# Low halves of the second weight matrix: one VectorE operation in place of a scaled copy on ScalarE and a subtraction on GpSimd

## The chip, the core and the metric

The kernel runs on one core of a Trainium2 chip. The metric is device time in microseconds (us) of one execution, the median of several runs. The engines are named as in the profile: PE (TensorE, matmuls), PEld (its weight loads), DVE (VectorE), ACT (ScalarE), POOL (GpSimd), SP (SyncE, which issues all DMAs here). Each engine works through its own queue in order; semaphores make one wait for another.

## The reference

Local and global attention, then a Fourier mixing layer, then a two-layer network with residual:

```python
s_g  = scale * q_g @ k_all^T;  out_g = softmax(s_g) @ v_all          # 32 global rows
s_ll = where(|i-j| <= 32, scale * q_l @ k_l^T, -1e9)                 # 512 local rows, a band
out_l = softmax([scale * q_l @ k_g^T, s_ll]) @ [v_g, v_l]
x  = heads of [out_g, out_l] side by side                             # (8, 544, 512)
u  = x + real(fft(fft(x, axis=1), axis=2))
un = (u - mean(u)) / sqrt(var(u) + 1e-6)
out = u + max(un @ w_ch1, 0) @ w_ch2                                  # 512 -> 2048 -> 512
```

The weights are drawn in double precision (`w_ch1` is 512 x 2048, `w_ch2` 2048 x 512); there are 8 batches, 8 heads and a head width of 64.

## The kernel before, in words

**Number format.** PE multiplies float16. Each float32 operand is carried as two float16 tiles, a high half (the value rounded) and a low half (what the rounding left), and each product is the sum of three: high x high, high x low, low x high. So for most operands there are a scaling, a high half and a low half to make, on ACT, DVE or POOL.

**Stages.** Per pair of heads: load q, k, v, sum their absolute values for a scale (`sums`, `scales`, tile `z`), split them (`prep_mul`, `prep_hi`, `prep_lo`, `v_mul`, `v_hi`, `v_lo`), local scores on PE (`scores`, L398), mask with running minimum on DVE (`masked`, L408), exponential on ACT (`exps`, L417), split of the probabilities (`p_hi` on ACT, `p_lo` on POOL, L425), a transposing DMA (`turn`), values on PE (`values`, L446, L448), normalisation on DVE (`norm`). The global rows go the same way (`g_scores`, `g_max`, `g_exp`, ...). Per batch the Fourier mixing follows: rows are loaded, folded by symmetry (`d_tail`, `d_even` on DVE, `d_odd` on POOL), split (`d_hi`, `d_lo`, the latter L636 on DVE) and multiplied with tables on PE. Then the network runs in 17 blocks of 256 rows: statistics (`l_stats`), normalised rows and their halves (`l_un`, `l_lo`), a transposing DMA, 8 steps of `f_first` (L811), `f_hi` (ACT), `f_lo` (DVE, L820) and `f_second` (L830), and at the end `f_end` (DVE, L835), which adds the residual.

**The weights.** They come as 64-bit numbers, 32 tiles of 128 x 512, and are turned into float32 with bit operations on DVE (`w_abs`, `w_bits`), into tiles `wm`. `w_max`, `w_fold` and `w_scale` find scales, which are powers of two, in tile `wsc`. `w_split` makes the float16 halves of tile `i` of matrix `k` (0 for `w_ch1`, 1 for `w_ch2`, called w2) into `wh`: `w_hi` writes the high half on ACT (L252). For w1 POOL then scales the float32 tile (L259) and subtracts (L262). For w2 ACT scales it in place (L261) and POOL subtracts (L262). w2's tiles are called split 0 to split 15 here. The slots of `wm` and `wh` rotate in one pool of 18: the `wh` of a w2 split takes the place that `wm` had two splits before.

**The order.** Every piece of work has a time in a plan (`Plan.add`, in slots of one quarter of a head pair, with a rank inside a slot), and the whole program is written out in the order of these times; nothing reorders it afterwards. `w_split` of w2 has slot 33 to 48 with rank .75: in a slot it comes after the masks (.67) and the global maximum (.68), and in ACT's queue after nearly all of the slot's other work. From slot 37 on the steps of the network's first block are woven in. `f_second(0, fp)` is the first reader of w2's halves 2fp and 2fp + 1.

Of the kernel before, what the change touches and what calls it, by code (L numbers as in the profile page):

```python
# [13 lines left out]
AF = mybir.ActivationFunctionType  # L14
ALU = mybir.AluOpType
# [75 lines left out]
class Kern:  # L91
# [163 lines left out]
    def w_split(self, k, i):  # L255
        nc = self.nc
        f, s, w = self.w_hi(k, i)
        if k == 0:
            nc.gpsimd.tensor_mul(f, f, s.to_broadcast([P, 512]))  # L259
        else:  # L260
            nc.scalar.activation(f, f, AF.Copy, scale=s)  # L261
        nc.gpsimd.tensor_sub(w[:, 1], f, w[:, 0])  # L262

    def b_load(self, b):
# [774 lines left out]
```

## Time and profile before

| what | us |
|---|---|
| median of 3 runs (lowest, highest) | 1156.88 (1155.44, 1157.02) |
| the profiled execution's own time | 1152.42 |
| its span, first to last instruction | 1150.5 |
| PE busy | 962.0 (84%) |
| DVE busy | 708.7 (62%) |
| ACT busy | 633.6 (55%) |
| POOL busy | 575.1 (50%) |
| mean granted TensorE clock | 0.941 |

The profile is one execution. Its page gives busy time by engine, the span in 40 slices, the chain of work that ended last, and groups of instructions by source line; other views give the busy time in chosen stretches, the waits, and the single instructions in order of time. A row of such a timeline reads: start in us, duration in us, engine, line, operation, output and inputs, and in brackets the idle time of the engine before it with what ended that wait. A duration includes any time for which the instruction was held after its start. The average shares hide that the stages differ: w1's and w2's weights are prepared and the first batches' attention runs in the first 300 us, and the network's matmuls fill the rest.

### The profile page before, as it was taken

How to read it: one execution, taken by the hardware profiler on the slowest of the kernel's cores; microseconds unless marked ns; L12 is line 12 of the kernel's file. 1: busy time of each engine (PE TensorE's matmuls, PEld its weight loads, DVE VectorE, ACT ScalarE, POOL GpSimd, SP SyncE). 2: the span in 40 equal slices, each digit the busy share in tenths (PEclk: the TensorE clock that was granted, in tenths of full speed). 3: DMA queues.
4: the chain of work that ended last, by engine and by line, in shares of the span. 5: the costliest groups of instructions: out<-in, count | busy, mean ns of one | idle time of the engine just before them, and what ended most of it. 6: DMA issues, size and time to landing. Idle time of an engine off the chain costs nothing.

```text
span 1150.5 us, 25346 instructions
## 1 busy us (share of the span) xinstructions
PE 962.0 (84%) x9831; PEld 682.0 (59%) x9831; DVE 708.7 (62%) x1868; ACT 633.6 (55%) x1366; POOL 575.1 (50%) x728
## 2 busy tenths in 40 slices
PE   0244226588799899999999999999999999999996
PEld 0133215465576677676766676767677666666664
DVE  6997798547866865686568656866584444413211
ACT  5768558888676656665666566656564213212210
POOL 3789375778656554665465546654573312201100
PEclk9996557699899999999999999999999999999999
DMA  7578966567387465747465746573646212011100
GB/s 267 151 152 225 276 157 141 112 135 170 75 179 151 108 167 91 141 115 165 93 138 118 170 88 143 112 179 72 135 79 130 60 58 65 24 46 38 19 19 19
DMA packets 249569, 137.63 MB, mean 120 GB/s; under 512 B 200576, under 2 KB 223200, under 8 KB 249448
## 3 DMA queue, kind: packets, MB, share of 16 engines
q1 hardware_dynamic: 249448, 136.01, 51.2%
q8 instruction: 77, 1.26, 0.5%
q14 instruction: 44, 0.36, 0.1%
HBM read 65.10 MB, written 18.35 MB: 73 GB/s over the span
## 4 chain that ended last, share of the span: by engine, by line
PE 55%; DVE 24%; ACT 8%; DMA 6%; POOL 4%; issue 2%; SPq 0%; DVEq 0%; POOLq 0%; ACTq 0%
PE ps L811 22%; PE acc L830 22%; PE S L398 2%; DMA xt<-xs 2%; ACT pe L417 2%; DVE pe L408 2%; DMA qk<-in_qk 2%; PE bk L707 2%; DVE h L820 1%; PE S L468 1%; DVE ps L195 1%; DVE ps L196 1%; DVE z L328 1%; DVE wm L197 1%; DVE ps L194 1%
## 5 line engine op out<-in xcount | busy, mean ns | idle before, releaser
L811 PE MATMUL ps<-uh,wh 128*128 128x256 f16 x3264 | 383.4, 275 | 0.0
L830 PE MATMUL acc<-wh,h 128*128 128x512 f16 x1632 | 377.3, 381 | 4.1 <-DVE u L835 2.9
L811 PEld LDWEIGHTS <-wh 128*128 128x128 f16 x3264 | 319.2, 99 | 59.4 <-issue 0.7
L830 PEld LDWEIGHTS <-h 128*128 128x128 f16 x1632 | 153.5, 99 | 174.1 <-issue 9.2
L820 DVE SCALAR_TENSOR_TENSOR h<-ps,h 128x512 f16<-128x512 f32 x136 | 93.3, 686 | 188.6 <-ACT h L816 188.0
L425 POOL TENSOR_TENSOR ph<-pe,ph 128x448 f16<-128x448 f32 x128 | 137.2, 1072 | 143.0 <-ACT ph L421 88.5
L816 ACT ACTIVATE h<-ps 128x512 f16<-128x512 f32 x136 | 80.2, 589 | 223.4 <-PE ps L811 223.3
L417 ACT ACTIVATE pe<-pe,nm 128x224 f32<-128x224 f32 x256 | 102.0, 469 | 72.1 <-DVE nm L408 71.8
L408 DVE CUSTOM_DVE_ANT_0 pe<-S,msk,z 128x224 f32<-128x224 f32 x256 | 99.6, 445 | 7.5 <-PE S L398 3.6
L446 PE MATMUL bk<-vN,pl 128*128 128x65 f16 x768 | 72.9, 203 | 31.9 <-DMA pl<-ph 10.0
L398 PE MATMUL S<-kT,qT 64*128 64x192 f16 x768 | 55.7, 269 | 44.1 <-ACT pg L482 37.5
L398 PEld LDWEIGHTS <-qT 64*128 64x128 f16 x1536 | 53.7, 101 | 49.7 <-issue 38.9
L446 PEld LDWEIGHTS <-pl 128*128 128x128 f16 x768 | 62.2, 104 | 23.9 <-DMA pl<-ph 18.4
L421 ACT ACTIVATE ph<-pe 128x448 f16<-128x448 f32 x128 | 72.0, 562 | 0.0
L448 PEld LDWEIGHTS <-pl 96*128 96x128 f16 x768 | 60.1, 104 | 17.3 <-issue 10.5
L764 POOL TENSOR_SCALAR ve<-ve 128x2 f32<-128x2 f32 x17 | 5.8, 339 | 113.3 <-DVE ve L763 113.1
L376 POOL TENSOR_TENSOR kT<-qk,kT 128x512 f16<-128x512 f32 x32 | 40.7, 1272 | 36.4 <-ACT kT L371 33.0
L723 DVE SCALAR_TENSOR_TENSOR asm<-bk,dsc,asm 128x258 f32<-128x258 f32 (+1 forms) x21 | 10.1, 482 | 75.1 <-PE bk L707 60.5
L448 PE MATMUL bk<-vB,pl 96*128 96x65 f16 x576 | 55.2, 204 | 0.0
L774 ACT ACTIVATE un<-u,ve 128x512 f32<-128x512 f32 x34 | 27.6, 811 | 47.7 <-DVE unh L779 37.7
L361 ACT ACTIVATE qk<-qk,z 128x512 f32<-128x512 f32 x64 | 45.2, 708 | 10.7 <-DVE z L326 10.7
L262 POOL TENSOR_TENSOR wh<-wm,wh 128x512 f16<-128x512 f32 x32 | 38.0, 1188 | 19.7 <-ACT wm L261 18.3
(188 smaller groups left out, 1654.8 us busy)
## 6 DMA issues: line engine op xcount, KB each, us to landing
qk<-in_qk SPq DMA_DIRECT2D x32, 512.0 KB
vf<-in_v SPq DMA_DIRECT2D x32, 320.0 KB
raw<-in_moe_w_ch SPq DMA_DIRECT2D x18, 512.0 KB
xs<-x SPq DMA_DIRECT2D x32, 256.0 KB
out<-u SPq DMA_DIRECT2D x16, 512.0 KB
rw<-in_moe_w_ch SPq DMA_DIRECT2D x12, 512.0 KB
x<-xs SPq DMA_DIRECT2D x24, 256.0 KB
u<-xs SPq DMA_DIRECT2D x24, 256.0 KB
```

Of the source, the lines that this page charges most:

```text
L361: self.nc.scalar.activation(s[nm], s[nm], AF.Copy, scale=s["z"][:, 3:4] if nm == "q" else s["z"][:, 4:5])
L398: nc.tensor.matmul(ps, qT[r, a, j], k, start=m == 0, stop=m == 2)
L408: nc.vector.tensor_tensor_reduce(self.per[(4 * p + j) % 4][:, h, 0:224], S[:, h, 224 * n:224 * n + 224], self.msk[:, j], z[:, 8:9], 3e38, ...
L417: nc.scalar.activation(pe[:, h, 0:224], pe[:, h, 0:224], AF.Exp, bias=nm[:, n, h:h + 1], scale=-1.0)
L421: self.nc.scalar.activation(ph[:, 0, :, 0:224], self.per[i % 4][:, :, 0:224], AF.Copy)
L425: self.nc.gpsimd.tensor_sub(ph[:, 1, :, 0:224], self.per[i % 4][:, :, 0:224], ph[:, 0, :, 0:224])
L446: nc.tensor.matmul(pv[:, j % 2, h], pl[:, 4 * a + 2 * h], vN[:, j, c, h, :], start=m == 0, stop=False)
L448: nc.tensor.matmul(pv[:, j % 2, h], pl[0:96, 4 * a + 2 * h + 1], vb, start=False, stop=m == 2)
L811: nc.tensor.matmul(ps[:, q], wt[:, w, c0:c0 + P], uh[:, :, 4 * a + kt, :], start=n == 0, stop=n == 11)
L816: self.nc.scalar.activation(h[:, 0], self.fps, AF.Relu)
L820: self.nc.vector.scalar_tensor_tensor(h[:, 1], self.fps, 0.0, h[:, 0], op0=ALU.max, op1=ALU.subtract)
L830: nc.tensor.matmul(self.acc_f[j], h[:, a, q, j * P:(j + 1) * P], self.w[1, f][:, w, :], start=f == 0 and a == 0 and w == 0, stop=f == 15 a ...
```

## The change

For w2 alone, the low half is made in one operation on DVE, `(f * s) - hi`, from the float32 tile, the scale and the high half. The scaled copy in place on ACT and the subtraction on POOL are no longer made. The high half on ACT and all of w1 stay.

```diff
         if k == 0:
             nc.gpsimd.tensor_mul(f, f, s.to_broadcast([P, 512]))
         else:
-            nc.scalar.activation(f, f, AF.Copy, scale=s)
+            nc.vector.scalar_tensor_tensor(w[:, 1], f, s, w[:, 0], op0=ALU.mult, op1=ALU.subtract)
+            return
         nc.gpsimd.tensor_sub(w[:, 1], f, w[:, 0])
```

In the changed kernel every line after the change has a number higher by one (L262 for w1 is L263 there, L820 is L821).

Three places show what moves. On POOL, the stretch around splits 1 and 2, before the change (kT is the low half of k, vN of v, ph of the probabilities):

```order
L732 TENSOR_TENSOR xm<-xm,asm 15x255
L262 TENSOR_TENSOR wh<-wm,wh 128x512
L425 TENSOR_TENSOR ph<-pe_89,ph 128x2x224
L262 TENSOR_TENSOR wh<-wm,wh 128x512
L376 TENSOR_TENSOR kT_66<-qk,kT_66 128x512
L351 TENSOR_TENSOR vN<-vf_76,vN 128x5x2x64
L425 TENSOR_TENSOR ph<-pe_86,ph 128x2x224
L791 TENSOR_TENSOR ve<-ve 128x2
```

and with it:

```order
L733 TENSOR_TENSOR xm<-xm,asm 15x255
L426 TENSOR_TENSOR ph<-pe_89,ph 128x2x224
L377 TENSOR_TENSOR kT_66<-qk,kT_66 128x512
L352 TENSOR_TENSOR vN<-vf_76,vN 128x5x2x64
L426 TENSOR_TENSOR ph<-pe_86,ph 128x2x224
L792 TENSOR_TENSOR ve<-ve 128x2
```

The two subtractions are gone, and the rest stands as it was. On DVE, splits 3 and 4 with the change (dng and xg are the normalisation of global rows, h the low half of the network's inner layer, dn of local rows):

```order
L261 SCALAR_TENSOR_TENSOR wh<-wm,wsc,wh 128x512
L512 TENSOR_SCALAR dng<-bk_127,z 64x1
L513 RECIPROCAL dng<-dng 64x1
L514 TENSOR_SCALAR xg<-bk_127,dng 64x64
L261 SCALAR_TENSOR_TENSOR wh<-wm,wsc,wh 128x512
L821 SCALAR_TENSOR_TENSOR h<-ps_2449,h 128x512
L458 TENSOR_SCALAR dn<-bk_128,z 128x4
```

Before, the same rows followed each other without the two L261. Last, on DVE at splits 13 and 14, in the folding of the second batch for its Fourier mixing (st, xt, et, x) and the global maximum (ng):

```order
L261 SCALAR_TENSOR_TENSOR wh<-wm,wsc,wh 128x512
L644 TENSOR_TENSOR st<-xt 32x255
L645 TENSOR_TENSOR xt<-xt 32x255
L646 TENSOR_TENSOR et<-xt 32x129
L647 TENSOR_TENSOR et<-xt 32x128
L648 TENSOR_TENSOR et<-st 32x128
L649 TENSOR_TENSOR et<-st 32x128
L598 TENSOR_TENSOR x_3160<-x_3160 128x4x255
L600 TENSOR_TENSOR x_3160<-x_3160 128x2x257
L475 TENSOR_REDUCE ng<-S 64x1
L476 TENSOR_REDUCE ng<-S 64x1
L477 TENSOR_SCALAR ng<-ng,z 64x1
```

Split 13's operation now stands ahead of the folding, and split 14's comes right behind the last of these rows.

## The prediction

> **What bounds the kernel now.** First the table of busy time by stretch (columns: stretch in us, length, busy us and instructions of PE, PEld, DVE, ACT, POOL, then granted clock, DMA share, GB/s), cut where w2's sixteen tiles are split.
>
> ```profile
> 200.00:220.00 20.00, 6.96 (x91) 5.43 (x92) 13.12 (x42) 14.94 (x29) 13.16 (x16) 0.57 0.68 134
> 220.00:240.00 20.00, 17.58 (x229) 13.57 (x224) 7.68 (x30) 19.36 (x42) 16.90 (x26) 0.92 0.62 143
> 240.00:260.00 20.00, 16.89 (x176) 11.66 (x175) 12.19 (x37) 16.15 (x37) 13.77 (x14) 0.91 0.49 106
> 260.00:280.00 20.00, 19.64 (x237) 14.36 (x235) 13.88 (x45) 18.47 (x39) 16.51 (x25) 1.00 0.67 160
> 280.00:300.00 20.00, 12.67 (x124) 8.14 (x124) 17.46 (x29) 16.38 (x36) 18.52 (x18) 0.83 0.49 93
> 400.00:600.00 200.00, 194.94 (x2103) 138.38 (x2101) 131.12 (x360) 123.58 (x277) 111.22 (x147) 0.99 0.59 127
> ```
>
> From 400 us on PE is busy 97% of the time (194.94 of 200): nothing but PE sets the pace there, and what arrives earlier at that stage ends earlier. From 200 to 300 us it is otherwise. The five rows sum to 73.7 us of PE, 64.3 of DVE, 85.3 of ACT and 78.9 of POOL in 100 us. ACT is the fullest, POOL next, and PE stands idle for 26 us. Next, the two instructions that the change takes away (duration minimum/median/maximum, first and last start).
>
> ```profile
> L261 ACT ACTIVATE wm<-wm,wsc x16: 721/722/724, 207.4 to 295.4; 128x512 f32<-128x512 f32 x16
>   POOL wh L262: 18.3, 9
> L262 POOL TENSOR_TENSOR wh<-wm,wh x32: 1145/1157/2151, 32.0 to 296.2; 128x512 f16<-128x512 f32 x32
> ```
>
> All sixteen L261 lie in that stretch, and in 9 cases POOL's subtraction L262 stood still until its L261 was done, 18.3 us together. So ACT's scaled copy holds up ACT's own queue and POOL's. Last, the chain that ended last, in order of time: two of its stretches.
>
> ```profile
> 217.43 0.72 ACT wm L261
> 218.15 0.67 ACT pg L481
> ...
> 219.13 1.30 PE S L398 x19
> ...
> 230.43 0.72 ACT wm L261
> ```
>
> The copy stands on the path that sets the end, ahead of the scores that PE waits for.
>
> **The change part by part.** It removes 16 L261 on ACT (16 x 0.722 = 11.6 us busy) and 16 L262 on POOL (16 x 1.157 = 18.5 us), and adds 16 operations on DVE, each f*s - hi from two SBUF tiles, 128x512 f32 to f16. That operation with these operands is in the profile: L636, the lower half of the DFT input.
>
> ```profile
> L636 DVE SCALAR_TENSOR_TENSOR eh<-s,dsc,eh x8: 732/744/1525, 173.2 to 957.8; 128x512 f16<-128x512 f32 x8
> 299.37 1.05 DVE L636 SCALAR_TENSOR_TENSOR eh<-x,dsc,eh 128x514 f16<-128x514 f32 x1
> 299.83 1.49 POOL L425 TENSOR_TENSOR ph<-pe,ph 128x448 f16<-128x448 f32 x1
> ```
>
> Alone it takes 0.74 us; its longest took 1.53. The two rows under it show why: DVE's operation overlaps POOL's, both are long. I take 1.0 us as the price of one, between 0.74 and 1.53, nearer the lower since POOL loses a quarter of its work here; 16 us of DVE in all, bounds 11.9 and 24.4. DVE goes from 64 to about 80 us in 100. [...]
>
> What is saved on the path, stretch by stretch. (A) Before 219 us:
>
> ```profile
> 217.43 0.72 ACT L261 ACTIVATE wm<-wm,wsc 128x512 f32<-128x512 f32 x1
> 218.06 0.76 ACT L481 ACTIVATE pg<-S,ng,z 64x512 f32<-64x512 f32 x1
> 218.29 1.15 POOL L262 TENSOR_TENSOR wh<-wm,wh 128x512 f16<-128x512 f32 x1 [2.77 <-ACT wm L261]
> ```
>
> From start to start the copy costs ACT 218.06 - 217.43 = 0.63 us; the exponential behind it releases PE's scores. Gain 0.63. The earlier splits 0 and 1 fall where ACT still waits on DVE, and I count nothing: split 0's new operation stands ahead of the DFT chain on DVE (+0.74), but L734 below is slow, most likely beside POOL's L340 of that time, which moves away when the L262 ahead of it goes.
>
> ```profile
> L733 DVE TENSOR_TENSOR xf<-xf,asm 18x257 f32<-18x257 f32 x8 | 3.7, 463 | 0.0
> 209.69 1.46 DVE L734 TENSOR_TENSOR xf<-xf,asm 18x255 f32<-18x255 f32 x1
> ```
>
> Its sister L733 of two more columns has a mean of 0.46 us (the upper row: busy us, mean ns); so 1.46 - 0.46 = 1.0 can come back there. Bounds -0.3 to +1.0 net.
>
> (B) From 219 to 245 us. POOL is behind, and PE waits for POOL:
>
> ```profile
> 226.12 1.15 POOL L262 TENSOR_TENSOR wh<-wm,wh 128x512 f16<-128x512 f32 x1
> 227.24 1.15 POOL L376 TENSOR_TENSOR qT<-qk,qT 128x512 f16<-128x512 f32 x1
> 228.45 0.26 PE L398 MATMUL S<-kT,qT 64*128 64x192 f16 x2 [2.10 <-POOL qT L376]
> ```
>
> POOL loses two L262 ahead of this qT (at 218.29, with its 2.77 us of waiting, and at 226.12): up to 2.77 + 2 x 1.15 = 5.1 us, of which some is spent on waiting for ACT's ph in between. More than 2.10 stays, and PE's wait goes. PE's gain is at most 0.63 + 2.10 = 2.7 at 229 us. ACT has to follow: three copies in its unbroken row between 224.7 and 239 us, one of them the 230.43 of the chain above, give 3 x 0.63 = 1.9. The smaller holds: B = 1.9. DVE has room: it is busy 7.68 of 20 us there, and splits 3 to 7 stand in its gaps. If ACT did not follow at all (its exponentials wait for DVE's masks), B would be 0; with all of PE's wait it is 2.1.
>
> (C) 246 to 252 us, where DVE makes z, ten tiny operations, and PE waits 3.1 us for them:
>
> ```profile
> 246.51 0.17 DVE L315 TENSOR_SCALAR z<-bk 128x6 int32<-128x6 int32 x1 [4.30 <-PE bk L244]
> 248.43 1.15 POOL L262 TENSOR_TENSOR wh<-wm,wh 128x512 f16<-128x512 f32 x1 [0.23 <-ACT wm L261]
> 248.60 1.01 DVE L330 TENSOR_SCALAR z<-z 128x4 f32<-128x4 f32 x1
> 252.57 0.35 PE L244 MATMUL bk<-accg,part 128*128 128x2 f32 x2 [3.11 <-DVE xg L513]
> ```
>
> L330 on four columns takes 1.01 us and ends at 249.61 with that L262 at 249.58: it is held by it. Without L262 it shrinks to something like L315's 0.17 on six columns, or another POOL operation takes its place. Between 0 and 0.84 comes back; C = 0.6. Split 7 stands before z in DVE's queue, but DVE idles 4.30 us ahead of z.
>
> (D) 267 to 290 us: POOL's ph, the turning DMAs behind it, the DFT's tail on DVE, then PE.
>
> ```profile
> 281.07 1.21 POOL L262 TENSOR_TENSOR wh<-wm,wh 128x512 f16<-128x512 f32 x1
> 281.19 1.24 DVE L646 TENSOR_TENSOR et<-xt 32x128 f32<-32x128 f32 x1
> 282.24 2.40 POOL L593 TENSOR_TENSOR s<-x 128x1020 f32<-128x1020 f32 x1
> 285.82 2.15 POOL L262 TENSOR_TENSOR wh<-wm,wh 128x512 f16<-128x512 f32 x1
> 286.99 1.53 DVE L599 TENSOR_TENSOR x<-x 128x514 f32<-128x514 f32 x1
> 290.64 0.66 PE L398 MATMUL S<-kT,qT 64*128 64x192 f16 x6 [6.04 <-ACT pg L482]
> ```
>
> Two L262 share their time with DVE's tail. L646 on 128 columns takes 1.24 beside the first; the second meets L599. Without them L593 starts about 1.2 earlier, and with it everything down to PE's 6.04 us of idleness. Against it split 13's new operation now stands ahead of the tail (+0.74 to 1.53). D between 0 and 2.4; I take 1.5, as POOL's part counts twice, once in its queue and once in what it blocks.
>
> (E) Costs. Split 10 follows the maximum of the global scores on DVE and waits for ACT's high half; behind it in DVE's queue are the layer statistics. Split 14 stands ahead of DVE's busiest row (289 to 296 us), with the masks that ACT's exponentials need behind it. Together +0.3, bounds -0.6 (POOL's operation is gone there too) to +2.0. Split 15 lies in a gap that ends at ACT's relu:
>
> ```profile
> 298.76 0.69 DVE L820 SCALAR_TENSOR_TENSOR h<-ps,h 128x512 f16<-128x512 f32 x1 [2.22 <-ACT h L816]
> ```
>
> Sum: 0.63 + 1.9 + 0.6 + 1.5 - 0.3 = 4.3 us. The profiled execution goes from a span of 1150.5 to 1146.2, and its own time from 1152.42 to 1148.1. The median of the runs, 1156.88, is 4.5 us above the profiled execution; with the same distance the forecast is **1152.6 us**. After 310 us neither queue differs from before, so the gain is handed on whole.
>
> **The rivals.** (1) *Nothing to measure.* 0.2% is 2.3 us, about what a measurement of this kernel tells from no change. It comes out so if the pieces do not add: PE restarts at 290.64 on DVE's tail, whose input comes by DMA, and if that does not move, A to C are waited away there. For it: 6.04 us of PE idleness at one place. Against it: those DMAs follow POOL's and ACT's work and move with it. Only D without its DMA part and E remain: gain 0.5 to 1.5, about 1156 us.
>
> (2) *Slower: DVE becomes the bound.* The place is 280 to 307 us, where DVE is busy 17.46 of 20 and PE waits for its last row, u:
>
> ```profile
> 307.23 2.75 PE L830 MATMUL acc<-wh,h 128*128 128x512 f16 x12 [2.86 <-DVE u L835]
> ```
>
> Splits 13, 14 and 15 fall there. At 1.53 each they add 4.6 us, and POOL, blocked in turn, hands its delay to the next DVE operation; with A to C (3.1) kept and D lost, the end is 1.5 later, with B lost too 3.4 later: 1160 us. With D lost it decides from a price of 3.1 / 3 = 1.0 each on, if none of the three finds a gap. [...]
>
> (3) *Much faster.* ACT's whole 16 x 0.63 = 10.1 us comes back, or the clock helps: the first 24 matmuls after PE's long waits are slow,
>
> ```profile
> 253.60 4.46 PE L811 MATMUL ps<-uh,wh 128*128 128x256 f16 x24
> 229.02 2.79 PE L811 MATMUL ps<-uh,wh 128*128 128x256 f16 x24
> ```
>
> 4.46 against 2.79 us, 1.7 for each wait that becomes short enough not to show this. At 253 and 291 us that would be 3.3 on top of 4.3: 1149 us. Against it: PE is busy 19.64 of 20 from 260 to 280 us, where ACT's saving is worth nothing.
>
> That the change does not do what it says can be set aside: the orders show one operation for two at all sixteen places and nothing else moved.
>
> **How the numbers follow.** The forecast, a gain of 2.3 to 7 us, has 0.50; rival 3 (over 7 us) 0.16; rival 1 0.22; rival 2 (over 2.3 us slower) 0.12. Faster is 0.50 + 0.16 = 0.66. The range goes from a gain of 10.1 (1147) to a loss of 1.6 (1158.5), which leaves out the ends of rivals 2 and 3, some 2 in 10. The forecast's own range is 1150 to 1154.5.
>
> **What would show it.** In the profile after: 16 rows of L261 on DVE with a median of 0.75 to 1.0 us and a longest near 1.5; ACT's busy time from 633.6 to 622, POOL's from 575 to 557, DVE's from 709 to 725 or so. The wait of 2.10 for qT at 228 us should be gone, and the first scores after it some 2.5 us earlier; PE's wait for z near 252 and its 6 us near 290 should be shorter. The same L811 rows shifted by 4 us at 400 us and at the end would show that the gain is handed on. I am wrong if PE's start after 290 us has not moved, if the new rows average over 1.53 us, or if DVE waits for ACT's high halves with masks queued behind.

## The result and the profile after

The changed kernel is faster: a median of 1146.38 us (6 runs, 1142.78 to 1151.48) against 1157.4 us for the kernel before (6 runs), a ratio of 0.9916 with a 95% interval of 0.9892 to 0.9940. Timed once more beside three experiments, on the same chip as they, it had 1149.83 us (5 runs) and a ratio of 0.9947 (0.9921 to 0.9973). All 11 runs together have a median of 1148.1. By the two ratios the gain is 6 to 10 us, and single executions differ by up to 9 us. The profiled execution has a span of 1140.9 us, 9.6 less than that of before, and is the fastest of the eleven. The profile of before was fast for its kernel too (1152.42 us against a median of 1157.4), so a difference of two single profiles is not the gain.

Busy time by stretch of the changed kernel (columns as in the prediction), with its line of busy time for each engine:

```profile
PE 962.4 (84%) x9831; PEld 683.1 (60%) x9831; DVE 715.2 (63%) x1884; ACT 622.1 (55%) x1350; POOL 558.9 (49%) x712
...
200.00:220.00 20.00, 7.71 (x99) 6.05 (x99) 15.28 (x43) 13.21 (x26) 12.50 (x15) 0.50 0.61 137
220.00:240.00 20.00, 19.59 (x229) 14.38 (x227) 12.89 (x43) 18.33 (x43) 14.40 (x22) 0.91 0.68 148
240.00:260.00 20.00, 18.44 (x229) 14.03 (x229) 14.04 (x40) 15.83 (x38) 9.98 (x10) 1.00 0.56 122
260.00:280.00 20.00, 17.41 (x204) 11.88 (x199) 16.82 (x46) 16.62 (x36) 16.55 (x24) 1.00 1.01 196
280.00:300.00 20.00, 14.37 (x168) 10.77 (x168) 18.53 (x39) 11.79 (x24) 14.94 (x13) 0.83 0.13 26
```

Over the whole execution ACT has 11.5 us less and POOL 16.2. DVE has only 6.5 more, though the new operations take 13.5: DVE's other work is held less. From 200 to 300 us PE is busy 77.5 us instead of 73.7. The new operations on DVE (duration minimum/median/maximum; then the group with busy us, mean ns, idle time before it):

```profile
L261 DVE SCALAR_TENSOR_TENSOR wh<-wm,wsc,wh x16: 734/751/1310, 208.4 to 289.5; 128x512 f16<-128x512 f32 x16
  PE acc L831: 0.2, 1
L261 DVE SCALAR_TENSOR_TENSOR wh<-wm,wsc,wh 128x512 f16<-128x512 f32 x16 | 13.5, 845 | 4.7 <-ACT wh L252 4.7
```

Their mean is 0.845 us, and PE waits for one of them once, for 0.2 us.

PE's timeline, at the places where the prediction has PE wait:

```profile
218.37 0.67 PE L399 MATMUL S<-kT,qT 64*128 64x192 f16 x6 [2.50 <-ACT pg L483]
226.46 2.79 PE L812 MATMUL ps<-uh,wh 128*128 128x256 f16 x24
236.60 0.42 PE L399 MATMUL S<-kT,qT 64*128 64x192 f16 x6 [0.41 <-ACT pg L483]
248.56 0.35 PE L244 MATMUL bk<-accg,part 128*128 128x2 f32 x2 [1.56 <-DVE xg L514]
249.59 2.79 PE L812 MATMUL ps<-uh,wh 128*128 128x256 f16 x24
283.30 0.66 PE L399 MATMUL S<-kT,qT 64*128 64x192 f16 x6 [5.89 <-ACT pg L483]
299.35 2.75 PE L831 MATMUL acc<-wh,h 128*128 128x512 f16 x12 [2.17 <-DVE u L836]
```

Read against the rows of before: the scores came at 219.13 and come 0.76 us earlier, the matmuls of 229.02 2.56 earlier (the wait for qT is gone), the row of 252.57 4.01, of 290.64 7.34, and of 307.23 7.88 earlier. The gain builds up in steps, most of them at the places that were named, and not evenly with every copy that ACT no longer makes.

### The profile page after: what moved, and what is told of

The parts are those of the page before. It is cut to its first block, busy times and chain, and to the rows that moved or that the text cites. A ratio compares the mean times of both kernels' runs of the same rounds, so it can differ in the third digit from the quotient of the medians.

```text
span 1140.9 us, 25333 instructions
## 1 busy us (share of the span) xinstructions
PE 962.4 (84%) x9831; PEld 683.1 (60%) x9831; DVE 715.2 (63%) x1884; ACT 622.1 (55%) x1350; POOL 558.9 (49%) x712
## 4 chain that ended last, share of the span: by engine, by line
PE 51%; DVE 26%; ACT 7%; DMA 7%; issue 4%; POOL 3%; SPq 1%; DVEq 0%; POOLq 0%; ACTq 0%
PE acc L831 21%; PE ps L812 21%; DVE pe L409 2%; ACT pe L418 2%; PE S L399 2%; DMA xt<-xs 2%; DVE h L821 2%; PE bk L708 2%; DVE ps L195 1%; DVE z L329 1%; DVE ps L194 1%; DVE ps L196 1%; PE S L469 1%; DVE z L319 1%; DVE wm L197 1%
## 5 line engine op out<-in xcount | busy, mean ns | idle before, releaser
L812 PE MATMUL ps<-uh,wh 128*128 128x256 f16 x3264 | 382.5, 274 | 0.0
L812 PEld LDWEIGHTS <-wh 128*128 128x128 f16 x3264 | 318.8, 98 | 58.9 <-issue 0.6
L426 POOL TENSOR_TENSOR ph<-pe,ph 128x448 f16<-128x448 f32 x128 | 135.7, 1060 | 162.1 <-ACT ph L422 98.5
L821 DVE SCALAR_TENSOR_TENSOR h<-ps,h 128x512 f16<-128x512 f32 x136 | 93.3, 686 | 184.4 <-ACT h L817 183.9
L447 PEld LDWEIGHTS <-pl 128*128 128x128 f16 x768 | 62.2, 104 | 22.2 <-DMA pl<-ph 16.6
L352 POOL TENSOR_TENSOR vN<-vf,vN 128x640 f16<-128x640 f32 x32 | 46.7, 1459 | 2.2 <-ACT vN L348 2.2
```

Of the source, the lines that this page charges most:

```text
L352: self.nc.gpsimd.tensor_sub(vN[:, :, 1, :, 0:64], self.st[p]["vf"], vN[:, :, 0, :, 0:64])
L426: self.nc.gpsimd.tensor_sub(ph[:, 1, :, 0:224], self.per[i % 4][:, :, 0:224], ph[:, 0, :, 0:224])
L447: nc.tensor.matmul(pv[:, j % 2, h], pl[:, 4 * a + 2 * h], vN[:, j, c, h, :], start=m == 0, stop=False)
L812: nc.tensor.matmul(ps[:, q], wt[:, w, c0:c0 + P], uh[:, :, 4 * a + kt, :], start=n == 0, stop=n == 11)
L821: self.nc.vector.scalar_tensor_tensor(h[:, 1], self.fps, 0.0, h[:, 0], op0=ALU.max, op1=ALU.subtract)
```

## The experiments

My theory after the result, P: what counts is POOL's queue, which loses 1.16 us per split, and what its subtractions take from DVE. The rival, A: ACT was the fullest engine from 200 to 300 us, so its copy carries the gain. A third, D: DVE is the new bound, and the operations on it cost. All ratios are to the kernel before, from executions on the same chip.

**ACT's part put back**

```diff
+            nc.scalar.activation(self.junk[:, 0:512], f, AF.Copy, scale=s)
             nc.vector.scalar_tensor_tensor(w[:, 1], f, s, w[:, 0], op0=ALU.mult, op1=ALU.subtract)
```

> The change with ACT's scaled copy of each w2 tile put back, into a tile that nobody reads, so that only ACT's share of the saving is undone (16 x 0.7 us). The profiled span fell from 1150.5 to 1140.9, a gain of 9.6 us. Theory P (POOL's queue and what its subtractions block carry most of the gain): before the scores at 218 us 0.6 to 0.8 is lost, near 236 us PE is held by ACT again and some 2 us are lost, and the rest stays, so a gain of 6 to 8 us remains. Theory A (ACT was the fullest engine, its copy carries the gain): most is lost, a gain of 0 to 4 us remains.

1150.65 us, ratio 0.9947 (0.9929 to 0.9965): a gain of 6 us is left, as theory P has it. Beside the 0.9916 of the first timing the copy is worth 3.6 us, beside the 0.9947 of the second nothing. In this kernel's profile ACT holds PE again at the scores which waited 0.41 us with the change:

```profile
240.35 0.42 PE L400 MATMUL S<-kT,qT 64*128 64x192 f16 x6 [2.17 <-ACT pg L484]
```

So the copy has a price at this place; how much of the whole gain it is, the medians leave open between 0 and 4 us.

**POOL's part put back**

```diff
+        self.pj = c.tile([P, 512], F16, name="pj")
 ...
             nc.vector.scalar_tensor_tensor(w[:, 1], f, s, w[:, 0], op0=ALU.mult, op1=ALU.subtract)
+            nc.gpsimd.tensor_sub(self.pj, f, w[:, 0])
```

> The change with POOL's subtraction put back, into a tile that nobody reads and without the wait for the scaled copy: only POOL's share of the saving is undone (16 x 1.16 us). Theory P: POOL is late again for qT at 226 us, and its operations again block DVE's z near 245 us and the folding near 280 us; most of the 9.6 us is lost, a gain of 0 to 4 us remains. Theory A: POOL only needed to be rid of its waits for ACT, which stay away; a gain of 6 to 9 us remains.

1156.92 us, ratio 1.0000 (0.9984 to 1.0016): the whole gain is gone, with ACT's copy still away. Theory A falls: the copy's absence alone gains nothing. The run does not price POOL's part by itself, though, since with the subtraction back DVE's new operations take 1.21 us in the mean instead of 0.845. PE's waits from 200 to 320 us show why (us in total, times, longest):

```profile
PE S L401 <- POOL qT L379: 3.1, 1, 3.1
PE bk L245 <- DVE xg L516: 2.7, 1, 2.7
```

The wait for qT is back, 3.1 us, and the one for z with 2.7 as well.

**Three possible reasons why POOL's subtraction costs.** It takes POOL's time (20.5 us for the sixteen in this profile); it waits for ACT's high half (12.6 us); and it reads beside DVE. Two more kernels take these apart. The first puts POOL's time back with two memsets, which read nothing and wait for nobody:

```diff
+        self.pj = c.tile([P, 660], F16, name="pj")
 ...
+            for _ in range(2):
+                nc.gpsimd.memset(self.pj, 0.0)
```

> The change with POOL's time of the subtraction put back, but as two memsets of 660 float16 columns into a tile that nobody reads (about 0.6 us each by the 1.0 us that memsets of 1152 columns take in the trace): they read nothing and wait for nobody. With the subtraction itself put back the whole gain went. If it is POOL's time alone (its queue is late for what PE waits for): the gain of 9 to 10 us shrinks to 0 to 3. If it is what the subtraction takes from DVE by reading beside it, or its wait for ACT's high half: 6 to 10 us remain.

The second subtracts the float32 tile from itself, so it reads but does not wait:

```diff
+        self.pj = c.tile([P, 512], F16, name="pj")
 ...
+            nc.gpsimd.tensor_sub(self.pj, f, f)
```

> The change with a subtraction on POOL put back that reads only the float32 tile, twice, which is ready long before: POOL's time and its reads beside DVE are there, the wait for ACT's high half is not. Together with the memsets it tells the three apart. If the wait was the cause: 6 to 10 us of the gain remain here. If reading beside DVE: this one loses the gain, and the memsets do not. If POOL's time: both lose it, 0 to 3 us remain.

The memsets: 1152.13 us, ratio 0.9966 (0.9948 to 0.9985). The subtraction without a wait: 1156.34 us, ratio 0.9995 (0.9977 to 1.0013). Both ran 10 times; the slowest with the memsets had 1155.2, the fastest of the other 1153.8. The added rows on POOL, the memsets first, and under each the page's line of its kernel:

```profile
L264 POOL MEMSET pj<- x32: 638/648/651, 204.0 to 292.7; 128x660 f16 x32
PE 966.1 (84%) x9831; PEld 684.0 (60%) x9831; DVE 718.1 (62%) x1884; ACT 622.3 (54%) x1350; POOL 578.6 (50%) x744
```

```profile
L263 POOL TENSOR_TENSOR pj<-wm x16: 1030/1039/2416, 205.8 to 300.7; 128x512 f16<-128x512 f32 x16
PE 963.4 (83%) x9831; PEld 683.3 (59%) x9831; DVE 731.6 (63%) x1884; ACT 622.8 (54%) x1350; POOL 579.7 (50%) x728
```

The memsets take more of POOL (32 x 0.648 = 20.7 us) than the subtractions (16 x 1.04 = 16.6 at their median), and cost less. They leave DVE at 718.1 us of busy time, near the change's 715.2; the subtractions raise it to 731.6, with the same work on DVE. PE's wait for z, the first row with the memsets, the second with the subtraction:

```profile
PE bk L245 <- DVE xg L517: 1.9, 1, 1.9
```

```profile
PE bk L245 <- DVE xg L516: 5.5, 1, 5.5
```

So the wait for the high half was not the cause; of the 6 to 10 us some 2 to 6 are POOL's time (against the two timings of the change; the 2 is not clear of noise), and about 4 (1156.34 - 1152.13) what the subtraction, which reads, takes from DVE and the memsets do not, by way of the rows that PE waits for (z: 5.5 us against 1.9). The intervals of the two runs overlap a little (0.9977 to 0.9985), so the size of this last part is rough. One more reason would be that the subtraction keeps its input tiles in use for longer. It can be set aside: in neither of the two profiles with a subtraction put back does anything wait for that subtraction.

**DVE's part doubled, made with one input, and taken away.** The operation made twice:

```diff
             nc.vector.scalar_tensor_tensor(w[:, 1], f, s, w[:, 0], op0=ALU.mult, op1=ALU.subtract)
+            nc.vector.scalar_tensor_tensor(w[:, 1], f, s, w[:, 0], op0=ALU.mult, op1=ALU.subtract)
```

> The change with DVE's new operation made twice, so 16 more of 0.75 to 1.3 us. If the new operations lie in gaps of DVE (theory P), at most 4 of them stand on the path (splits 0, 8, 10, 14): 2 to 4 us slower than the change, a gain of 5.5 to 7.5 us over the kernel before remains. If DVE sets the pace from 207 to 300 us after the change (my rival 2 come late), each counts: 16 x 0.75 = 12 us or more, and the kernel is slower than before.

With one input tile only:

```diff
+        self.pj = c.tile([P, 1], F32, name="pj")
 ...
-            nc.vector.scalar_tensor_tensor(w[:, 1], f, s, w[:, 0], op0=ALU.mult, op1=ALU.subtract)
+            nc.vector.tensor_scalar(w[:, 1], f, s, None, op0=ALU.mult, op1=ALU.max, accum_out=self.pj)
```

> The change with DVE's new operation replaced by one of the same size with a single tile as input (f * s with a running maximum), which leaves out the subtraction of the high half: w2's low halves are then not the low halves. It measures what the second input costs, that is the share of the 16 operations in the contention with POOL. In the change their median is 0.75 and 3 or 4 of the 16 take 1.2 to 1.3. If the contention is worth little: all 16 at 0.69 or so, and the time within 1.5 us of the change. If it is a main cost left: 3 us or more faster than the change.

Not made at all:

```diff
-            nc.vector.scalar_tensor_tensor(w[:, 1], f, s, w[:, 0], op0=ALU.mult, op1=ALU.subtract)
 ...
-    nc.tensor.matmul(self.acc_f[j], h[:, a, q, j * P:(j + 1) * P], self.w[1, f][:, w, :],
+    nc.tensor.matmul(self.acc_f[j], h[:, a, q, j * P:(j + 1) * P], self.w[1, f][:, 0, :],
```

> The change without DVE's new operation: w2's low halves are not made at all, and PE reads the high half in their place (same matmuls, same sizes), so the part of the product with the low half is left out. It measures what all 16 new operations cost together. If they lie in gaps as I summed (0.3 us on the path): a gain of 9 to 11 us over the kernel before, that is within 2 us of the change. If every one counts as the 16 doubled ones did (10 us): a gain of 16 to 20 us.

Twice: 1156.87 us, ratio 1.0006 (0.9991 to 1.0022), the whole gain lost. One input: 1148.98 us, ratio 0.9920 (0.9895 to 0.9946). None: 1146.88 us, ratio 0.9928 (0.9904 to 0.9952). Neither expectation of the doubling came true: theory P left 5.5 to 7.5 us of the gain, and the rival made the kernel slower than before. In the medians the sixteen operations cost nothing that stands out of the noise (some 3 us, by the intervals), and sixteen more cost 7 to 10 us. The likeliest reading is that DVE's gaps behind the high halves hold one operation and not two. The second one of the doubled kernel, DVE's timeline at split 13, and PE's waits from 200 to 320 us:

```profile
L262 DVE SCALAR_TENSOR_TENSOR wh<-wm,wsc,wh x16: 750/752/2726, 209.5 to 300.3; 128x512 f16<-128x512 f32 x16
279.11 0.75 DVE L261 SCALAR_TENSOR_TENSOR wh<-wm,wsc,wh 128x512 f16<-128x512 f32 x1
279.89 2.73 DVE L262 SCALAR_TENSOR_TENSOR wh<-wm,wsc,wh 128x512 f16<-128x512 f32 x1
282.54 1.25 DVE L645 TENSOR_TENSOR st<-xt 32x255 f32<-32x255 f32 x1
PE acc L832 <- DVE wh L262: 4.3, 2, 2.8
```

PE waits for DVE's low halves, and the folding (L645) begins 282.54 - 279.86 = 2.7 us behind the end of the first of the two. With one input nothing is gained, but this run says little about the price of contention, since each operation is followed by a read of its accumulator:

```profile
L262 DVE TENSOR_SCALAR_CACHE_REDUCE wh<-wm,wsc x16: 727/734/744, 210.0 to 293.0; 128x512 f16<-128x512 f32 x16
L262 DVE DVE_READ_ACCUMULATOR wh<-wm,wsc x16: 74/78/86, 210.7 to 293.7; 128x1 f32 x16
```

Together the sixteen take 16 x (0.734 + 0.078) = 13.0 us, against 13.5 in the change.

**By splits.** The new way for some of the splits alone (the first kernel; the second has `i < 7` in place of `i > 6`):

```diff
         if k == 0:
             nc.gpsimd.tensor_mul(f, f, s.to_broadcast([P, 512]))
+        elif i > 6:
+            nc.scalar.activation(f, f, AF.Copy, scale=s)
         else:
```

> Splits 0 to 6 in the new way on DVE, splits 7 to 15 in the old way (copy on ACT, subtraction on POOL). By my terms A and B, which the profile after shows as 2.5 us near 236 us: a gain of 2 to 4 us over the kernel before. If the gain comes from the late splits alone: within 1.5 us of it.

> Splits 7 to 15 in the new way on DVE, splits 0 to 6 in the old way. By the shifts of the profile after (2.5 us before 240 us, 7.1 us after it): a gain of 5 to 7 us over the kernel before, and with early_half about the whole. If the late splits meet DVE where it is fullest and cost there: a gain under 3 us.

Splits 0 to 6: 1154.07 us, ratio 0.9985 (0.9971 to 1.0000). Splits 7 to 15: 1151.34 us, ratio 0.9955 (0.9936 to 0.9974). In their medians 2.2 and 4.9 us, the second just under the 5 that were expected. That is near the split that the steps of PE's timeline show (2.5 before 240 us, of which 1.0 was there ahead of the first split, and the rest after it), and the sum of 7.1 lies inside what the whole gives.

**w1 as well**

```diff
-        if k == 0:
-            nc.gpsimd.tensor_mul(f, f, s.to_broadcast([P, 512]))
-        else:
-            nc.vector.scalar_tensor_tensor(w[:, 1], f, s, w[:, 0], op0=ALU.mult, op1=ALU.subtract)
-            return
-        nc.gpsimd.tensor_sub(w[:, 1], f, w[:, 0])
+        nc.vector.scalar_tensor_tensor(w[:, 1], f, s, w[:, 0], op0=ALU.mult, op1=ALU.subtract)
```

> The change for w1 as well: POOL's scaling and its subtraction (1.04 and 1.16 us) of each w1 tile go, and DVE makes the low half (16 x 0.75 or more) between 30 and 112 us. DVE is busy 46 of 50 us there and POOL 44 of 50. If DVE's bit operations on the arriving weights set the pace of that stage: each counts, 5 to 12 us slower than the change. If POOL does: 3 to 8 us faster than the change.

1151.23 us, ratio 0.9958 (0.9937 to 0.9979): not faster than the change, and beside its first timing 5 us slower. In the profiles the loss lies where w1 is prepared: from PE's row at 37 us to its row at 203 us this kernel takes 203.85 - 37.23 = 166.6 us, the two profiles of the change 202.02 - 36.78 = 165.2 and 201.73 - 36.89 = 164.8. So DVE's gaps there seem to be too small for the new operations. The two timings of the change differ by 3.5 us, so how much is lost is not settled.

**The change again, and a try at more.** The change once more as a measure, and with POOL's scaling of v on ACT for head pairs 3 to 7:

```diff
     def v_mul(self, p):
         s = self.st[p]
+        if 2 < p < 8:
+            self.nc.scalar.activation(s["vf"], s["vf"], AF.Copy, scale=s["sc"])
+            return
         self.mul(s["vf"], s["sc"])
```

> The change once more, beside the three others on the same chip, as their measure. All theories: a ratio of 0.990 to 0.994 to the kernel before, as first measured (0.9916).

> The change, and POOL's scaling of v (1.24 us) on ACT (about 0.65 us) for the five head pairs 3 to 7, whose work falls between 205 and 305 us. If POOL is what holds that stage, each us taken from it is worth about 10/18.5 = 0.54 and each us given to ACT costs about 4/11.6 = 0.35, by the two runs that put ACT's and POOL's parts back: 5 x (0.67 - 0.23) = 2 us faster than the change. If POOL no longer holds it: no gain, or up to 2 us slower.

Again: 1149.83 us, ratio 0.9947 (0.9921 to 0.9973). With v on ACT: 1146.92 us, ratio 0.9921 (0.9894 to 0.9948). The medians differ by 2.9 us in the expected direction, but the intervals overlap widely and the change's first timing was as good. Whether this is a better kernel stays open.

**The stage in every profile.** The same stage can be compared without the rest of the execution: from PE's row that starts at 203.01 us before, ahead of the first changed instruction, to the row at 307.23 us, behind the last. One profile each, in us from its start:

| kernel | first row | last row | between |
|---|---|---|---|
| before | 203.01 | 307.23 | 104.22 |
| the change | 202.02 | 299.35 | 97.33 |
| the change again | 201.73 | 300.48 | 98.75 |
| ACT's copy back | 203.32 | 305.42 | 102.10 |
| POOL's subtraction back | 202.52 | 309.70 | 107.18 |
| memsets on POOL | 202.59 | 303.60 | 101.01 |
| subtraction without a wait | 204.36 | 312.03 | 107.67 |
| DVE's operation twice | 202.34 | 309.45 | 107.11 |
| with one input | 203.63 | 303.01 | 99.38 |
| not made | 202.30 | 297.54 | 95.24 |
| splits 0 to 6 alone | 201.70 | 303.96 | 102.26 |
| splits 7 to 15 alone | 202.61 | 305.09 | 102.48 |
| w1 as well | 203.85 | 301.50 | 97.65 |
| v on ACT | 200.33 | 296.79 | 96.46 |

The clock alone moved such a length by 1.67 us in two executions of the same kernel (last section), so under 2 us nothing is told apart here. Most of it agrees with the medians; only splits 7 to 15, whose profile is the slowest of its ten, do not show their 4.9 us. Two things are clearer than in the medians. ACT's copy put back costs 3.4 and 4.8 us against the two profiles of the change. Without the sixteen operations the stage is 2.1 and 3.5 us shorter than in these two, so the operations are probably not quite free. Behind the last row the fourteen profiles have 841.6 to 849.2 us, in no order that follows from the kernels.

## Why the prediction came out as it did

The direction and the likeliest mechanism were right. The forecast of 4.3 us was too small: 6 to 10 us were measured, on both sides of the 7 us at which rival 3 begins.

- **A (0.63 before 219 us)** was right for the copy: PE's lead over the kernel before goes from 0.01 us (the PE rows below) to 0.76. What I counted as nothing ahead of it was not nothing. At 202.02 us, ahead of any changed instruction, PE had a lead of 0.99, and it lost this. POOL no longer waits for L261 there and scales v (L341) earlier, and beside it DVE's L780 takes 1.61 us instead of 0.69. The second profile of the change loses the same. First before, then with the change:

```profile
204.60 0.69 DVE L779 TENSOR_TENSOR unh<-un,unh 128x512 f16<-128x512 f32 x1 [1.64 <-ACT unh L775]
213.49 0.64 PE L468 MATMUL S<-kT,gT 128*64 128x512 f16 x1 [4.09 <-DVE nm L408]
```

```profile
203.41 1.25 POOL L341 TENSOR_TENSOR vf<-vf,z 128x640 f32<-128x640 f32 x1
203.60 1.61 DVE L780 TENSOR_TENSOR unh<-un,unh 128x512 f16<-128x512 f32 x1 [1.64 <-ACT unh L776]
213.48 0.64 PE L469 MATMUL S<-kT,gT 128*64 128x512 f16 x1 [4.16 <-DVE nm L409]
```

- **B (1.9 up to 239 us)** was right, with its limit. A and B made 2.53; the matmuls after qT's wait come 2.56 earlier and the scores near 237 us 2.47 earlier, with 0.41 of waiting for ACT. Putting POOL's subtraction back brought the wait for qT back, and putting ACT's copy back the wait for ACT: both limits were real.
- **C (0.6 at z)** is the mis-sized term. PE's row behind z gained another 4.01 - 2.46 = 1.55: its wait fell from 3.11 to 1.56. I counted one operation that POOL held, L330 with 1.01 us, and reckoned that another POOL operation might take the place of L262. The profile before has three more that were held (the shortest of sixteen take 0.17, 0.17 and 0.22 us at these lines):

```profile
247.02 1.21 DVE L318 TENSOR_SCALAR z<-z 128x4 int32<-128x4 int32 x1
249.65 1.18 DVE L331 TENSOR_SCALAR z<-z 128x4 f32<-128x4 f32 x1
250.74 1.07 DVE L332 TENSOR_SCALAR z<-z,ge 128x2 f32<-128x2 f32 x1
```

  With the change POOL's row ended earlier as a whole, so that DVE was held once, for 2.15 us (L319's shortest takes 0.17), up to the end of POOL's L426, and then was free:

```profile
243.43 1.27 POOL L489 TENSOR_TENSOR pgr<-pg,pgr 64x576 f16<-64x576 f32 x1
244.66 1.25 POOL L341 TENSOR_TENSOR vf<-vf,z 128x640 f32<-128x640 f32 x1
244.78 2.15 DVE L319 TENSOR_SCALAR z<-z 128x4 int32<-128x4 int32 x1
245.88 1.03 POOL L426 TENSOR_TENSOR ph<-pe,ph 128x448 f16<-128x448 f32 x1
246.97 0.16 DVE L329 SCALAR_TENSOR_TENSOR z<-z 128x2 f32<-128x2 f32 x1
```

  Behind z the matmuls L812 took 2.79 instead of 4.46, 1.67 us which I had put into rival 3. That part is chance, as the last section argues.
- **D (1.5 from 267 to 290 us)** came out at 7.34 - 5.68 = 1.66, where 5.68 is 4.01 + 1.67. The sum is right, one reason for it is not. DVE's folding is still held beside POOL, now by the DFT's own subtraction (L594) and by kT: L646 takes 2.33 us and L600 1.53, their shortest of eight 0.28 and 0.70. It begins 280.08 - 273.82 = 6.26 us earlier, 0.58 more than PE's lead of 5.68, and from its first row to the end of L600 (L599 before, in the prediction's fence) it takes 7.35 us instead of 8.44: the other 1.09. First before, then with the change:

```profile
280.08 0.41 DVE L643 TENSOR_TENSOR st<-xt 32x255 f32<-32x255 f32 x1 [0.62 <-DMA xt<-xs]
```

```profile
273.82 0.41 DVE L644 TENSOR_TENSOR st<-xt 32x255 f32<-32x255 f32 x1
274.36 2.54 POOL L594 TENSOR_TENSOR s<-x 128x1020 f32<-128x1020 f32 x1
274.71 2.33 DVE L646 TENSOR_TENSOR et<-xt 32x129 f32<-32x129 f32 x1
277.89 2.73 POOL L377 TENSOR_TENSOR kT<-qk,kT 128x512 f16<-128x512 f32 x1
279.64 1.53 DVE L600 TENSOR_TENSOR x<-x 128x514 f32<-128x514 f32 x1
```

- **E (a cost of 0.3)** had the wrong sign in this pair of profiles: 7.88 - 7.34 = 0.54 gained. My price of 1.0 us per operation was measured as 0.845, and the kernel without the operations shows no cost of all sixteen in its median, and 2 to 3.5 us in its stage. The margin was narrow, which I did not see: twice the operations lose everything. Rival 2 (DVE the bound) did not come, but the doubling shows that it was near.
- **"The gain is handed on whole"** can't be read from single profiles, and the medians only do not contradict it. Between two executions of the same changed kernel the part behind 293 or 295 us differs: 1140.9 - 293.3 = 847.6 and 1149.7 - 294.6 = 855.1 us, where the numbers 293.3 and 294.6 are the starts of the same L812 row. PE's waits in the rows below, from 312 us to the end, for the first profile and then for the second, show part of it.

```profile
PE S L399 <- ACT pg L483: 5.1, 3, 3.0
```

```profile
PE S L399 <- ACT pg L483: 11.2, 4, 3.3
```

  So of the 9.6 us between the two spans 7.88 were there at 307 us and 1.7 came behind. Of the 7.88, 0.99 was there ahead of the change's first place and 1.67 came by the clock, which leaves 5.2 for the change. The second profile has 307.23 - 300.48 = 6.75 there, with a lead of 203.01 - 201.73 = 1.28 ahead of the change and without the clock's help behind z: 5.5. Why the medians show up to 10 us stays open.
- **Rival 1** (the pieces do not add) is refuted by D: the folding moved with the rest.
- **What POOL's operations take from DVE** depends on the operation: DVE was busy 718.1 us with memsets on POOL and 731.6 with a subtraction, which reads. Operations on DVE with two input tiles were held (the new one: median 0.751, longest 1.310), and the short ones on z with one input tile as well (L319 above, 2.15 us). Why POOL's operations hold them was not shown by any run. Work moved from POOL to DVE gained 6 to 10 us here, against rival 2: two passes on two engines became one, and DVE had gaps.

## What to carry to other kernels

Look for what the waiting engine waits for, not for the fullest one: ACT was busiest here, but taking its copy away gained nothing while POOL's subtraction stayed, because POOL's results were late (PE waited 2.10 us for qT before the change, and 3.1 with the subtraction back) and its subtractions held the short DVE operations that PE waits for (L330 on z: 1.01 us beside one, its shortest 0.17). With the subtraction gone, ACT's copy counted too. An operation put into an engine's gaps can cost little until the gaps are full: here sixteen cost nothing that the medians show, and sixteen more 7 to 10 us. Doubling it on the chip tells how far that is. And where executions differ by 9 us, two single profiles name the places, but only medians give the size.

## What the runs showed of the hardware

The granted clock differed between two executions at the same place, after the same wait: 1.00 in one, 0.50 in the other. These are the first and the second profile of the changed kernel, with PE's row behind z (the wait for z was 1.56 us in both) and stretches of about 3.41 us around it; PE's busy time is the first number behind the length, the clock the third from the end:

```profile
249.59 2.79 PE L812 MATMUL ps<-uh,wh 128*128 128x256 f16 x24
244.07:247.48 3.41, 2.93 (x24) 1.50 (x22) 3.27 (x6) 1.81 (x4) 2.83 (x3) 1.00 0.73 125
247.48:250.90 3.42, 2.34 (x38) 2.20 (x39) 3.22 (x13) 1.12 (x3) 0.97 (x2) 1.00 0.11 25
250.90:254.31 3.41, 3.41 (x36) 2.42 (x35) 1.98 (x9) 3.17 (x8) 0.97 (x1) 1.00 0.69 152
```

```profile
249.31 4.46 PE L812 MATMUL ps<-uh,wh 128*128 128x256 f16 x24
246.20:249.60 3.40, 1.84 (x42) 1.67 (x41) 3.19 (x14) 1.12 (x3) 0.48 (x2) 1.00 0.26 45
249.60:253.00 3.40, 3.40 (x18) 2.42 (x17) 2.93 (x13) 2.15 (x6) 0.90 (x2) 0.50 0.61 130
```

In the clock records of the profiles before and after, every spell of one value but the last lasts 3.41 us or a multiple of it (after: 3.41, 6.83, 30.72, 58.03, 88.75 us and so on). The stretches of the first execution are cut on multiples of 3.41 us from a change of its clock at 223.6 us, those of the second where its spell of half the clock begins. In the second execution the whole wait falls into one stretch, PE is busy 1.84 of 3.40 us there, and the next stretch has a clock of 0.50: 24 matmuls take 4.46 - 2.79 = 1.67 us longer. In the first the wait falls across two stretches, with 2.93 and 2.34 us of PE, and the clock stays at 1.00. So in the second execution this wait of PE had its length and 1.67 us on top, in the first its length alone. Six profiles have a wait of 1.55 or 1.56 us at this place. Behind it the 24 matmuls took 2.79 us in three of them (the change, low halves not made, v on ACT) and 4.46 in the other three (the change again, one input, w1 as well). This was read from these traces, which do not show what sets the clock, and not tried by an experiment of its own; it is one source of the spread between executions.

The second thing is how differently POOL's operations treat DVE: with sixteen subtractions of 1.04 us, which read a float32 tile, DVE was busy 731.6 - 718.1 = 13.5 us longer at the same work than with 32 memsets of 0.65 us.
